# GpSimd makes the sign and tail bits of converted weights, VectorE joins them in one step; reciprocals go into x; two buffers for keys-values

## The chip, the cores and the metric

The kernel runs on one core of a Trainium2 chip. The metric is the time of one execution on the device in microseconds (us). The engines are named as in the profile: PE is TensorE (PEld its weight loads), DVE is VectorE, ACT is ScalarE, POOL is GpSimd, SP is SyncE, from whose queue all DMA transfers start.

## The reference

Attention with random features for 8 batches of 8 heads, sequence 576, head size 64, 128 features, and on its output a dense layer pair with an unusual gate:

```python
def phi(x):                       # for q and k, both scaled by 64 ** -0.25
    proj = einsum('bhsd,md->bhsm', x, omega)
    h = proj - sum(x * x, -1) / 2
    return exp(h - max(h, -1)) / sqrt(128)
q_p, k_p = phi(q), phi(k)
kv  = einsum('bhsm,bhsd->bhmd', k_p, v)
z   = sum(k_p, 2)
out = (q_p @ kv) / (q_p @ z + 1e-6)          # per head

x = out.transpose(0, 2, 1, 3).reshape(4608, 512)
h = x @ w_in                                  # 512 x 2048
g = h * erf(softplus(h))
y = g @ w_out                                 # 2048 x 512
```

The two weight matrices arrive as float64.

## The kernel before

**Order of the work.** `build` does not write instructions; it lists operations (`pl.op`) with the tiles that they read and write, the engines that may run them (T for PE, A, V, G, S), a cost for each, and for some a planned time. `Plan.order` then plays these costs through a list scheduler on the host and so fixes one order for each engine, in which the instructions are issued. An operation starts on an engine when its inputs are ready, its tiles find a free buffer (`SLOTS` per pool, `CAPS` per stream) and it is the one with the earliest due time. The third number of an option is a limit: an engine takes the operation only while its due time is at least so far away (-1e9: always). So `GATES0 = 10` and `RESTS0 = 15` mean that in the first batches GpSimd takes the work called gate only if it is due in 10 us or later and rest only in 15 or later; VectorE takes both always. On PE, matmuls with 64 rows (names that begin with proj) and key-values (kv, 64 columns) form groups: after one of these, another of the same kind that is due within `NEAR = 12` us goes first, if its tiles have room (lines 236 to 241). One PSUM bank holds one `ps` tile; there are eight, and the attention stream may hold six (`att=6`).

**Attention.** It goes by pairs of heads, 32 in all. The first four pairs are done singly (`first`), the others two pairs at a time (`attention`, 14 times), spread over the dense layers of the batch before. For two pairs: three projections of keys (tile `ppk`, nine chunks of 128 rows in three groups; each group takes two banks), maximum on VectorE (`sqk`, `mxk`), exponential on ScalarE (`fk`), then both pairs' key-values (`kvp`), then the same for queries (`ppq`, `fq`), transposes (`pt` to `qh`, `ql`), and the matmuls `nd`, which give numerator and denominator. The squares of q and k (`unq`, `unk`) are squared and folded mostly on GpSimd. Key-values are copied out of PSUM to `kh` and, from pair 12 on (counted from 0), their rest to `kl`; each has one buffer. Last (`attend`), ScalarE takes the reciprocal of the denominator by Ln and Exp into `rc` (two buffers), and VectorE multiplies the numerator by it into `xs` (four buffers, 128 multiplications of 64x288).

**Float32 in two parts.** Matmuls after attention run on pairs of reduced-precision numbers, a high part and the rest, three matmuls for a product (`xh`, `xl`; `gh`, `gl`; the two halves of `w`). From batch 2 on, the first dense layer uses a Strassen-like scheme with seven products and sums of weights (`R`, `S`, `cS`).

**Weights.** There are 32 units of 128x512 weights. `make` loads one as 64-bit words (tile `st`, low and high 32 bits), turns it into float32 by handling the bits, splits it into high part and rest (tile `w`) and stores it to DRAM (`wdw`), from which later uses fetch it. The steps for a unit before the change:

- `w_bias` on GpSimd or ScalarE: the high word, read as float32, times 2^-112, into tile `wt` (in SBUF);
- `w_shift` on VectorE: `wt` shifted left by 3 into the PSUM tile `pw`;
- `w_sign` and `w_tail` on VectorE, both in place on `pw`: the sign bit of the high word and the top three bits of the low word are put in;
- `w_high` (ScalarE or VectorE) and `w_rest` (VectorE): the two parts.

`pw` has one bank (`PW = 1`). `wt` lies in the pool of the tiles `gh`, whose buffers have room for 4,608 bytes per partition.

Of the kernel before, what the change touches and what calls it, by code (L numbers as in the profile page):

```python
# [10 lines left out]
F32 = mybir.dt.float32  # L11
F32R = mybir.dt.float32r
I32 = mybir.dt.int32
AF = mybir.ActivationFunctionType
ALU = mybir.AluOpType
AX = mybir.AxisListType
# [3 lines left out]
P = 128  # L20
# [7 lines left out]
T = 288  # L28
# [7 lines left out]
HW = 2 * BW  # L36
# [21 lines left out]

COST = dict(mm=0.132, proj=0.224, turnout=0.40, tr=0.109, kv=1.08, table=1.3)
LAG = {"T": 0.35, "A": 0.35, "V": 0.33, "G": 0.33, "S": 0.3}  # L60
SLOTS = dict(w=8, u=2, un=2, f=2, mx=2, sq=2, v=2, qh=1, ql=1, kh=1, kl=1, rc=2, xs=4, xh=2, xl=2, u2=2,
             hs=4, gs=2, gh=6, gl=6, os=4, ps=8)
CAPS = dict(st=2, wt=2, cv=2, att=6, moe1=3, moe2=2)

# [25 lines left out]
class Plan:  # L90
# [44 lines left out]
    def order(self, slots, caps):  # L135
# [46 lines left out]
        def can(o):  # L182
            for t in o.uses:
                if t.slot is None and t.users[0] is not o:
                    return False
            more, room = {}, {}
            for t in o.alloc:
                k = more.get(t.stream, 0)
                stream = self.streams[t.stream]
                if stream[min(nxt[t.stream] + k, len(stream) - 1)] is not t:  # L190
                    return False
                if len(free[t.pool]) <= room.get(t.pool, 0):
                    return False
                if held[t.stream] + k >= (t.cap or caps.get(t.stream, 99)):
                    return False
                more[t.stream], room[t.pool] = k + 1, room.get(t.pool, 0) + 1
            return True
# [5 lines left out]
        while True:  # L203
            progress = True
            while progress:
                progress = False
                for e in engines:
# [28 lines left out]
                    if e == "T" and half and chosen.half != half:  # L236
                        near = [x for x in ready[e] if x[2].half == half and x[2].start is None
                                and x[0] < now + NEAR and can(x[2])]
                        if near:
# [95 lines left out]
EARLYB = 7  # L335
PW = 1
WHV = 0.0
GATES0 = 10.0
RESTS0 = 15.0
SQA = 4.0  # L340
NEAR = 12.0
KV1 = 0.15
GROUPS = ((0, 3), (3, 6), (6, 9))
WHG = 5.0
WBG = -1e9


def build(emit):

    pl = Plan()  # L350
    E = emit
# [17 lines left out]
    def when(n, x):  # L369
        return pair_time(n, x) if n < NP else quad_time(n // 2, x)  # L370

    xh, xl = {}, {}
# [26 lines left out]
    def make(u, t):  # L399

        nm = "_".join(str(c) for c in u)
        st = pl.tile("gl", f"st{nm}", [P, HW, 2], I32, "st")
        pl.op("wload", [("S", 0.1, AHEAD)], lambda e: E.w_load(st, u),
              writes=[(st, 0), (t, "room")], size=P * HW * 8)
        w = pl.tile("gh", f"wt{nm}", [P, HW], I32, "wt")
        pl.op("wbias", [("G", 0.65, WBG), ("A", 0.6, -1e9)], lambda e: E.w_bias(e, st, w),
              reads=[(st, 0)], writes=[(w, 0)])

        p = pl.tile("ps", f"pw{nm}", [P, HW], I32, "pw", PW)
        pl.op("wshift", [("V", 0.7, -1e9)], lambda e: E.w_shift(p, w), reads=[(w, 0)],  # L410
              writes=[(p, 0)])
        pl.op("wsign", [("V", 0.7, -1e9)], lambda e: E.w_sign(st, p), reads=[(st, 0), (p, 0)],
              writes=[(p, 0)])
        pl.op("wtail", [("V", 0.72, -1e9)], lambda e: E.w_tail(st, p), reads=[(st, 0), (p, 0)],
              writes=[(p, 0)])
        parts(t, lambda: p.ap.bitcast(F32).rearrange("p (k c) -> p k c", k=2), [(p, 0)], True)
        store(u, t)

    def unit(u, block=None):
# [3 lines left out]
                    [P, 2 if block is None else 1, 2, BW], F32R,  # L423
                    cap=SLOTS["w"] - CAPS["cv"] if clock[0] < starts[2 * PLAIN + 1] else None)
        if u not in stored:
# [45 lines left out]
    xs = {}  # L471
# [3 lines left out]
    def early(n):  # L475
        return EARLYB if n < NP else None
# [132 lines left out]
    def attend(n, t0):  # L609
        a = pairs[n]  # L610
        x = xs[n] = pl.tile("xs", f"xs{a['nm']}", [P, 2, T])
        for t in range(2):
            rc = pl.tile("rc", f"rc{a['nm']}_{t}", [P, T])
            nds = []
            for j in range(2):
                nd = pl.tile("ps", f"nd{a['nm']}_{j}_{t}", [P, 512], F32, "att", early(n))
                nds.append(nd)
                c = range((j * S + t * T) // 384, (j * S + (t + 1) * T - 1) // 384 + 1)
                pl.op("nd", [("T", 0.5 if n < WHOLE else 3 * COST["mm"], -1e9)],
                      lambda e, j=j, t=t, nd=nd: E.attend(nd, a["kh"], a["kl"], a["qh"], a["ql"], j, t),  # L620
                      reads=[(a["kh"], 0), (a["kl"], 0)] + [(a["qh"], i) for i in c]
                      + [(a["ql"], i) for i in c], writes=[(nd, 0)],
                      plan=when(n, t0 + 0.1 * t + 0.05 * j))
            opts = [("V", 0.93, -1e9), ("A", 1.45, RECIP)] if n < POW else [("A", 1.5, -1e9)]
            pl.op("recip", opts, lambda e, nds=nds, rc=rc: E.reciprocal(e, rc, nds),
                  reads=[(nd, 0) for nd in nds], writes=[(rc, 0)], set="exp")
            for j in range(2):
                pl.op("divide", [("V", 0.4, -1e9)],
                      lambda e, j=j, t=t, nd=nds[j], rc=rc: E.divide(x, nd, rc, j, t),
                      reads=[(nds[j], 0), (rc, 0)], writes=[(x, (j, t))])  # L630

    def split(b, c):

# [116 lines left out]
    def chain(b, ph, fps):  # L750
# [13 lines left out]
        for fp, g in zip(fps, gr):  # L764
            four = [(g["hs"], (i, t)) for i in range(2) for t in range(2)]
            pl.op("gate", [("V", 1.27, -1e9), ("G", 2.78, GATES if (b, ph) >= EARLY else GATES0)], lambda e, g=g: E.gate(e, g["gs"], g["hs"]),
                  reads=four + [(g["gs"], 0)], writes=four)
# [3 lines left out]
            g["gl"] = pl.tile("gl", f"gl{b}_{ph}_{fp}", [P, 2, 2, T], F32R, cap=4 if b < PLAIN or (b, ph) == (PLAIN, 0) else None)  # L771
            pl.op("rest", [("G", 2.95, RESTS if (b, ph) >= EARLY else RESTS0), ("V", 1.3, -1e9)],
                  lambda e, g=g: E.rest(e, g["gl"], g["hs"], g["gh"]),
# [66 lines left out]
def tile_attention_moe(ctx: ExitStack, tc: tile.TileContext, qT, kT, qN, kN, vP, omT, w1, w2, out):  # L840
# [6 lines left out]
    class InOrder:  # L847
# [5 lines left out]
        def __getattr__(self, name):  # L853
            method = getattr(self.engine, name)

            def call(*args, **kwargs):
# [3 lines left out]
    pe, act, dve, pool, sp = (InOrder(e) for e in (nc.tensor, nc.scalar, nc.vector, nc.gpsimd,  # L860
                                                   nc.sync))
# [10 lines left out]
    eps = const.tile([P, 1], F32, name="eps")  # L872
# [13 lines left out]
    def copy(e, dst, src):  # L886
        if e == "A":
            act.activation(dst, src, AF.Copy)
        elif e == "G":
# [15 lines left out]
    class Emit:  # L905
# [4 lines left out]
        def w_load(self, t, u):  # L910
            src = w1[u[1], u[2]] if u[0] == "1" else w2[u[1], u[2], u[3]]
            sp.dma_start(t.ap.rearrange("p a b -> p (a b)"), src.bitcast(I32))

        def w_bias(self, e, t, w):
            dst, src = w.ap.bitcast(F32), t.ap[:, :, 1].bitcast(F32)
            if e == "A":
                act.activation(dst, src, AF.Copy, scale=2.0 ** -112)
            else:
                pool.tensor_scalar(dst, src, 2.0 ** -112, 0.0, op0=ALU.mult, op1=ALU.add)

        def w_shift(self, p, w):
            dve.tensor_scalar(p.ap, w.ap, 3, None, op0=ALU.logical_shift_left)

        def w_sign(self, t, w):
            dve.scalar_tensor_tensor(w.ap, t.ap[:, :, 1], -2 ** 31, w.ap,
                                     op0=ALU.bitwise_and, op1=ALU.bitwise_or)

        def w_tail(self, t, w):
            dve.scalar_tensor_tensor(w.ap, t.ap[:, :, 0], 29, w.ap,
                                     op0=ALU.logical_shift_right, op1=ALU.bitwise_or)  # L930

        def w_high(self, e, t, src):
            copy(e, t.ap[:, :, 0, :], src())
# [21 lines left out]
        def pair_square(self, e, u, qk, i, parts):  # L955
# [5 lines left out]
            else:  # L961
                act.activation(u.ap[dst, c], u.ap[src, c], AF.Square)

# [17 lines left out]
        def square(self, e, un):  # L981
            if e == "A":
                act.activation(un.ap, un.ap, AF.Square)
            else:
# [27 lines left out]
        def exponential(self, parts):  # L1012
            for f, c, m, pp, k in parts:
                act.activation(f.ap[:, c, :], pp.ap[:, k * P:(k + 1) * P], AF.Exp, bias=m)

# [48 lines left out]
        def reciprocal(self, e, rc, nds):  # L1064

            for j, nd in enumerate(nds):
                num, den = rows(j)
                if e == "A":
                    act.activation(rc.ap[num], nd.ap[den, :T], AF.Ln, bias=eps[den])
                else:  # L1070
                    dve.tensor_scalar(rc.ap[num], nd.ap[den, :T], 1e-6 * P, -1.0, op0=ALU.add,
                                      op1=ALU.pow)
            if e == "A":
                act.activation(rc.ap, rc.ap, AF.Exp, scale=-1.0)

        def divide(self, x, nd, rc, j, t):
            num = rows(j)[0]
            dve.tensor_mul(x.ap[num, t, :], nd.ap[num, :T], rc.ap[num])

        def x_high(self, e, h, src, i, n):  # L1080
            copy(e, h.ap[:, i:i + n, :], src())
# [51 lines left out]
    plan = build(Emit())  # L1133
    slots = dict(SLOTS)
    for o in plan.ops:
# [60 lines left out]
```

## Time and profile before

| | us |
|---|---|
| median of 3 runs | 1037.3 |
| lowest and highest run | 1034.58, 1037.31 |
| the profiled execution | 1036.85 |
| its span, first to last instruction | 1035.1 |

| engine | busy us | share of the span | instructions |
|---|---|---|---|
| PE | 1015.7 | 98% | 8784 |
| DVE | 750.2 | 72% | 1488 |
| ACT | 686.9 | 66% | 1312 |
| POOL | 495.8 | 48% | 479 |

The mean granted clock of TensorE is 0.995 of full speed. Matmuls are pipelined and their ends are modelled, so PE counts as busy also where it runs below its best pace. In the groups of the profile all the instructions of the kernel have one line (the line that issues the planned operations), so that groups are told apart by tiles: `pw<-st,pw` is the step that writes `pw` from `st` and `pw`.

### The profile page before, as it was taken

What the parts mean: (1) busy time and instruction counts of PE and PEld (TensorE: products, weight loads), DVE (VectorE), ACT (ScalarE), POOL (GpSimd) and SP (SyncE); (2) the same over time, 40 slices, a digit from 0 to 9 for tenths busy, and PEclk for the clock granted to TensorE, in tenths of its full rate; (3) what the DMA queues carried; (4) which work ended last, traced back from release to release, by engine and by line L of the source; (5) the groups of instructions that cost most, each with busy time, mean ns of one, the idle gap of its engine ahead of it and who ended that gap; (6) DMA issues with size and microseconds to landing.
All of it is one profiled execution on the core that took longest, in us unless ns stands there. A gap on an engine that the chain in (4) does not pass through costs nothing.

```text
span 1035.1 us, 23091 instructions
## 1 busy us (share of the span) xinstructions
PE 1015.7 (98%) x8784; PEld 983.8 (95%) x8784; DVE 750.2 (72%) x1488; ACT 686.9 (66%) x1312; POOL 495.8 (48%) x479
## 2 busy tenths in 40 slices
PE   7989999999999999999999999999999999999998
PEld 6789899999999999999999999999999999999998
DVE  3989999989777577875777766776778756765531
ACT  7869959867786665777667666775668666453340
POOL 4637828969775233833446234652428312433310
PEclk9989999999999999999999999999999999999999
DMA  7675879789768686677777676778766756668861
GB/s 230 193 242 208 262 247 343 274 312 351 238 241 290 245 286 220 242 235 268 262 253 249 217 269 239 243 263 268 265 207 232 254 178 224 225 233 265 277 229 47
DMA packets 80142, 254.18 MB, mean 246 GB/s; under 512 B 8992, under 2 KB 9504, under 8 KB 80032
## 3 DMA queue, kind: packets, MB, share of 16 engines
q1 hardware_dynamic: 80032, 252.71, 71.3%
q8 instruction: 70, 1.15, 0.4%
q14 instruction: 40, 0.33, 0.1%
HBM read 218.07 MB, written 34.60 MB: 244 GB/s over the span
## 4 chain that ended last, share of the span: by engine, by line
PE 89%; DVE 5%; ACT 3%; issue 1%; DMA 1%; SPq 1%; POOL 0%; ACTq 0%; DVEq 0%
PE o L857 38%; PE hS L857 15%; PE hA L857 11%; PE h L857 9%; PE nd L857 4%; PE kvp L857 3%; PE ppk L857 3%; PE ppq L857 3%; PE pt L857 3%; DVE pw L857 1%; DVE xs L857 1%; DMA uq<-qT 1%; SPq L857 1%; DVE w L857 1%; ACT fq L857 1%
## 5 line engine op out<-in xcount | busy, mean ns | idle before, releaser
L857 PE MATMUL o<-gh,w 128*128 128x288 f32 x2048 | 446.2, 299 | 1.0 <-DVE w L857 0.9
L857 PEld LDWEIGHTS o<-gh,w 128*128 128x128 f32 x2048 | 338.7, 188 | 7.4 <-DVE w L857 1.4
L857 PE MATMUL o<-gl,w 128*128 128x288 f32 x1024 | 302.0, 295 | 0.0
L857 PEld LDWEIGHTS o<-gl,w 128*128 128x128 f32 x1024 | 192.7, 188 | 0.6 <-DVE gl L857 0.3
L857 POOL TENSOR_TENSOR hs<-gs,hs 128x576 f32<-128x576 f32 x70 | 107.5, 1557 | 169.8 <-ACT gs L857 126.2
L857 PE MATMUL hS<-xh,wS 128*128 128x288 f32 x768 | 187.8, 298 | 0.0
L857 POOL TENSOR_TENSOR gl<-hs,gh 128x576 fp32r<-128x576 f32 x84 | 138.0, 1668 | 40.1 <-ACT gh L857 31.0
L857 PE MATMUL hA<-xh,w 128*128 128x288 f32 x576 | 147.3, 297 | 0.0
L857 PEld LDWEIGHTS hS<-xh,wS 128*128 128x128 f32 x768 | 134.5, 188 | 0.7
L857 PE MATMUL h<-xh,w 128*128 128x288 f32 x512 | 120.0, 311 | 0.5 <-DVE w L857 0.2
L857 ACT ACT_TABLE_LOAD x92 | 118.0, 1283 | 2.4 <-PEq L1187 0.7
L857 POOL TENSOR_TENSOR unq<-unq 128x288 f32<-128x288 f32 (+2 forms) x63 | 50.3, 801 | 137.2 <-ACT unq L857 122.3
L857 PE MATMUL hS<-xl,wS 128*128 128x288 f32 x384 | 113.4, 295 | 0.0
L857 PEld LDWEIGHTS hA<-xh,w 128*128 128x128 f32 x576 | 103.2, 188 | 0.0
L857 ACT ACTIVATE fk<-ppk,mxk 128x128 f32<-128x128 f32 x288 | 77.3, 416 | 37.6 <-DVE mxk L857 37.4
L857 ACT ACTIVATE rc<-nd,eps 64x288 f32<-64x288 f32 x128 | 63.5, 496 | 54.5 <-PE nd L857 48.2
L857 PEld LDWEIGHTS h<-xh,w 128*128 128x128 f32 x512 | 86.9, 191 | 3.4 <-DVE w L857 0.7
L857 PE MATMUL hA<-xl,w 128*128 128x288 f32 x288 | 85.3, 296 | 0.0
L857 POOL TENSOR_TENSOR unk<-unk 128x144 f32<-128x144 f32 (+2 forms) x68 | 50.5, 747 | 70.9 <-DMA unk<-kN 50.5
L857 ACT ACTIVATE gs<-hs 128x1152 f32<-128x1152 f32 x64 | 72.4, 1162 | 18.1 <-DVE hs L857 17.5
L857 ACT ACTIVATE fq<-ppq,mxq 128x128 f32<-128x128 f32 x288 | 79.4, 392 | 6.4 <-DVE mxq L857 6.3
L857 PE MATMUL h<-xl,w 128*128 128x288 f32 x256 | 76.3, 298 | 0.0
(109 smaller groups left out, 2058.3 us busy)
## 6 DMA issues: line engine op xcount, KB each, us to landing
w<-wdw SPq DMA_DIRECT2D x176, 512.0 KB, 4.6
wS<-wdcS SPq DMA_DIRECT2D x96, 512.0 KB, 4.5
st<-w SPq DMA_DIRECT2D x32, 512.0 KB, 4.8
wdw<-w SPq DMA_DIRECT2D x32, 512.0 KB, 4.1
w<-wdw SPq DMA_DIRECT2D x48, 256.0 KB, 3.9
v<-vP SPq DMA_DIRECT2D x32, 325.0 KB, 6.2
out<-os SPq DMA_DIRECT2D x32, 288.0 KB, 3.8
wdcS<-cS SPq DMA_DIRECT2D x16, 512.0 KB, 4.6
```

What stands on the lines that cost most here:

```text
L857: return tc.keep_in_program_order(method(*args, **kwargs))
```

## The change

- **Weights.** `w_bias` runs on GpSimd alone. The new `w_tail` (GpSimd) reads the top byte of the low word and computes byte / 32 - 15.5 / 32, which rounds to the top three bits as a number, into the low int16 half of a second plane of `wt`; the new `w_sign` (GpSimd) writes 0 or -2^15 into the high int16 half. `w_shift` becomes one VectorE instruction: plane 0 shifted left by 3, or plane 1, into `pw`. `wt` is twice as long and still fits its buffer.
- **Reciprocals.** `rc` goes away; the reciprocal is written into the place in `xs` that the multiplication then overwrites.
- **Buffers.** `kh` and `kl` get two each.
- **Planner.** `GATES0` 10 to 3, `RESTS0` 15 to 5, `NEAR` 12 to 20, and the new operations' costs.

```diff
@@ -11,6 +11,8 @@
 F32 = mybir.dt.float32
 F32R = mybir.dt.float32r
 I32 = mybir.dt.int32
+U8 = mybir.dt.uint8
+I16 = mybir.dt.int16
 AF = mybir.ActivationFunctionType
 ALU = mybir.AluOpType
 AX = mybir.AxisListType
@@ -58,7 +60,7 @@
 
 COST = dict(mm=0.132, proj=0.224, turnout=0.40, tr=0.109, kv=1.08, table=1.3)
 LAG = {"T": 0.35, "A": 0.35, "V": 0.33, "G": 0.33, "S": 0.3}
-SLOTS = dict(w=8, u=2, un=2, f=2, mx=2, sq=2, v=2, qh=1, ql=1, kh=1, kl=1, rc=2, xs=4, xh=2, xl=2, u2=2,
+SLOTS = dict(w=8, u=2, un=2, f=2, mx=2, sq=2, v=2, qh=1, ql=1, kh=2, kl=2, xs=4, xh=2, xl=2, u2=2,
              hs=4, gs=2, gh=6, gl=6, os=4, ps=8)
 CAPS = dict(st=2, wt=2, cv=2, att=6, moe1=3, moe2=2)
 
@@ -335,14 +337,15 @@
 EARLYB = 7
 PW = 1
 WHV = 0.0
-GATES0 = 10.0
-RESTS0 = 15.0
+GATES0 = 3.0
+RESTS0 = 5.0
 SQA = 4.0
-NEAR = 12.0
+NEAR = 20.0
 KV1 = 0.15
 GROUPS = ((0, 3), (3, 6), (6, 9))
 WHG = 5.0
 WBG = -1e9
+WTAIL = (("G", 0.66, WBG),)
 
 
 def build(emit):
@@ -402,16 +405,16 @@
         st = pl.tile("gl", f"st{nm}", [P, HW, 2], I32, "st")
         pl.op("wload", [("S", 0.1, AHEAD)], lambda e: E.w_load(st, u),
               writes=[(st, 0), (t, "room")], size=P * HW * 8)
-        w = pl.tile("gh", f"wt{nm}", [P, HW], I32, "wt")
-        pl.op("wbias", [("G", 0.65, WBG), ("A", 0.6, -1e9)], lambda e: E.w_bias(e, st, w),
+        w = pl.tile("gh", f"wt{nm}", [P, 2, HW], I32, "wt")
+        pl.op("wbias", [("G", 0.65, WBG)], lambda e: E.w_bias(e, st, w),
               reads=[(st, 0)], writes=[(w, 0)])
+        pl.op("wtail", WTAIL, lambda e: E.w_tail(e, st, w),
+              reads=[(st, 0)], writes=[(w, 1)])
+        pl.op("wsign", [("G", 0.68, WBG)], lambda e: E.w_sign(st, w),
+              reads=[(st, 0)], writes=[(w, 2)])
 
         p = pl.tile("ps", f"pw{nm}", [P, HW], I32, "pw", PW)
-        pl.op("wshift", [("V", 0.7, -1e9)], lambda e: E.w_shift(p, w), reads=[(w, 0)],
-              writes=[(p, 0)])
-        pl.op("wsign", [("V", 0.7, -1e9)], lambda e: E.w_sign(st, p), reads=[(st, 0), (p, 0)],
-              writes=[(p, 0)])
-        pl.op("wtail", [("V", 0.72, -1e9)], lambda e: E.w_tail(st, p), reads=[(st, 0), (p, 0)],
+        pl.op("wshift", [("V", 0.7, -1e9)], lambda e: E.w_shift(p, w), reads=[(w, 0), (w, 1), (w, 2)],
               writes=[(p, 0)])
         parts(t, lambda: p.ap.bitcast(F32).rearrange("p (k c) -> p k c", k=2), [(p, 0)], True)
         store(u, t)
@@ -610,7 +613,6 @@
         a = pairs[n]
         x = xs[n] = pl.tile("xs", f"xs{a['nm']}", [P, 2, T])
         for t in range(2):
-            rc = pl.tile("rc", f"rc{a['nm']}_{t}", [P, T])
             nds = []
             for j in range(2):
                 nd = pl.tile("ps", f"nd{a['nm']}_{j}_{t}", [P, 512], F32, "att", early(n))
@@ -622,12 +624,12 @@
                       + [(a["ql"], i) for i in c], writes=[(nd, 0)],
                       plan=when(n, t0 + 0.1 * t + 0.05 * j))
             opts = [("V", 0.93, -1e9), ("A", 1.45, RECIP)] if n < POW else [("A", 1.5, -1e9)]
-            pl.op("recip", opts, lambda e, nds=nds, rc=rc: E.reciprocal(e, rc, nds),
-                  reads=[(nd, 0) for nd in nds], writes=[(rc, 0)], set="exp")
+            pl.op("recip", opts, lambda e, nds=nds, t=t: E.reciprocal(e, x.ap[:, t, :], nds),
+                  reads=[(nd, 0) for nd in nds], writes=[(x, (j, t)) for j in range(2)], set="exp")
             for j in range(2):
                 pl.op("divide", [("V", 0.4, -1e9)],
-                      lambda e, j=j, t=t, nd=nds[j], rc=rc: E.divide(x, nd, rc, j, t),
-                      reads=[(nds[j], 0), (rc, 0)], writes=[(x, (j, t))])
+                      lambda e, j=j, t=t, nd=nds[j]: E.divide(x, nd, j, t),
+                      reads=[(nds[j], 0)], writes=[(x, (j, t))])
 
     def split(b, c):
 
@@ -911,23 +913,26 @@
             src = w1[u[1], u[2]] if u[0] == "1" else w2[u[1], u[2], u[3]]
             sp.dma_start(t.ap.rearrange("p a b -> p (a b)"), src.bitcast(I32))
 
+        def scaled(self, e, dst, src, scale, bias):
+            if e == "A":
+                act.activation(dst, src, AF.Copy, scale=scale, bias=bias)
+            else:
+                pool.tensor_scalar(dst, src, scale, bias, op0=ALU.mult, op1=ALU.add)
+
         def w_bias(self, e, t, w):
-            dst, src = w.ap.bitcast(F32), t.ap[:, :, 1].bitcast(F32)
-            if e == "A":
-                act.activation(dst, src, AF.Copy, scale=2.0 ** -112)
-            else:
-                pool.tensor_scalar(dst, src, 2.0 ** -112, 0.0, op0=ALU.mult, op1=ALU.add)
+            self.scaled(e, w.ap[:, 0].bitcast(F32), t.ap[:, :, 1].bitcast(F32), 2.0 ** -112, 0.0)
+
+        def w_tail(self, e, t, w):
+            byte = t.ap.bitcast(U8).rearrange("p a b -> p (a b)")[:, 3::8]
+            self.scaled(e, w.ap[:, 1].bitcast(I16)[:, 0::2], byte, 1 / 32, -15.5 / 32)
+
+        def w_sign(self, t, w):
+            pool.tensor_scalar(w.ap[:, 1].bitcast(I16)[:, 1::2], t.ap[:, :, 1].bitcast(F32), 0.0, -2.0 ** 15,
+                               op0=ALU.is_lt, op1=ALU.mult)
 
         def w_shift(self, p, w):
-            dve.tensor_scalar(p.ap, w.ap, 3, None, op0=ALU.logical_shift_left)
-
-        def w_sign(self, t, w):
-            dve.scalar_tensor_tensor(w.ap, t.ap[:, :, 1], -2 ** 31, w.ap,
-                                     op0=ALU.bitwise_and, op1=ALU.bitwise_or)
-
-        def w_tail(self, t, w):
-            dve.scalar_tensor_tensor(w.ap, t.ap[:, :, 0], 29, w.ap,
-                                     op0=ALU.logical_shift_right, op1=ALU.bitwise_or)
+            dve.scalar_tensor_tensor(p.ap, w.ap[:, 0], 3, w.ap[:, 1], op0=ALU.logical_shift_left,
+                                     op1=ALU.bitwise_or)
 
         def w_high(self, e, t, src):
             copy(e, t.ap[:, :, 0, :], src())
@@ -1066,16 +1071,16 @@
             for j, nd in enumerate(nds):
                 num, den = rows(j)
                 if e == "A":
-                    act.activation(rc.ap[num], nd.ap[den, :T], AF.Ln, bias=eps[den])
+                    act.activation(rc[num], nd.ap[den, :T], AF.Ln, bias=eps[den])
                 else:
-                    dve.tensor_scalar(rc.ap[num], nd.ap[den, :T], 1e-6 * P, -1.0, op0=ALU.add,
+                    dve.tensor_scalar(rc[num], nd.ap[den, :T], 1e-6 * P, -1.0, op0=ALU.add,
                                       op1=ALU.pow)
             if e == "A":
-                act.activation(rc.ap, rc.ap, AF.Exp, scale=-1.0)
-
-        def divide(self, x, nd, rc, j, t):
+                act.activation(rc, rc, AF.Exp, scale=-1.0)
+
+        def divide(self, x, nd, j, t):
             num = rows(j)[0]
-            dve.tensor_mul(x.ap[num, t, :], nd.ap[num, :T], rc.ap[num])
+            dve.tensor_mul(x.ap[num, t, :], nd.ap[num, :T], x.ap[num, t, :])
 
         def x_high(self, e, h, src, i, n):
             copy(e, h.ap[:, i:i + n, :], src())
```

## The prediction

> **What bounds the kernel now.** I read the page first, then busy time by stretch, then the timeline and waits where TensorE pauses, then the chain of waits. Busy time on the page, and PE's, PEld's, DVE's, ACT's and POOL's in a stretch from the middle (start and end, length, busy time and count of each engine, granted clock, DMA share, GB/s):
>
> ```profile
> PE 1015.7 (98%) x8784; PEld 983.8 (95%) x8784; DVE 750.2 (72%) x1488; ACT 686.9 (66%) x1312; POOL 495.8 (48%) x479
> ```
> ```profile
> 400.00:500.00 100.00, 100.00 (x913) 97.55 (x912) 74.32 (x156) 66.82 (x135) 43.78 (x41) 1.00 0.74 250
> ```
>
> PE has 1035.1 − 1015.7 = 19.4 us idle in the whole span, and none in the middle. A freer VectorE is worth nothing there, unless PE itself executes less. Two places remain: the early part, where weights are made, and the price of PE's own order. The early part, 26 to 246 us, in which all 32 weight units are converted:
>
> ```profile
> 26.00:60.00 34.00, 28.63 (x266) 25.14 (x262) 32.84 (x68) 28.17 (x81) 22.30 (x30) 0.97 0.61 198
> 60.00:110.00 50.00, 49.94 (x431) 46.81 (x430) 44.52 (x94) 41.90 (x87) 30.64 (x33) 0.95 0.68 228
> 110.00:160.00 50.00, 48.33 (x443) 43.98 (x443) 47.05 (x91) 38.99 (x92) 27.45 (x33) 1.00 0.81 264
> 160.00:210.00 50.00, 49.44 (x409) 46.69 (x406) 47.71 (x73) 42.80 (x78) 43.79 (x39) 1.00 0.86 312
> 210.00:246.00 36.00, 36.00 (x357) 34.79 (x355) 31.29 (x62) 25.30 (x58) 26.73 (x29) 1.00 0.93 340
> ```
>
> VectorE is the fullest helper: 32.84 + 44.52 + 47.05 + 47.71 + 31.29 = 203.4 of 220 us, against 150.9 for GpSimd. PE is idle for 5.4 + 0.1 + 1.7 + 0.6 + 0 = 7.7 us. The clock costs more, which no idle column shows: 0.03 × 34 + 0.05 × 50 = 3.5 us of PE work. So the stretch can give back 11.2 us at most.
>
> Is VectorE the cause? Its timeline at the worst point, PE's longest waits in the first 70 us (total, times, longest), and two ten-microsecond stretches:
>
> ```profile
> 50.61 0.69 DVE L857 TENSOR_SCALAR pw<-wt 128x512 int32<-128x512 int32 x1
> 51.33 1.43 DVE L857 SCALAR_TENSOR_TENSOR pw<-st,pw 128x512 int32<-128x512 int32 x2
> 52.80 0.69 DVE L857 CAST w<-pw 128x512 fp32r<-128x512 f32 x1
> 53.52 0.69 DVE L857 TENSOR_TENSOR w<-pw,w 128x512 fp32r<-128x512 f32 x1
> 54.13 0.93 DVE L857 TENSOR_TENSOR xs<-nd,rc 64x288 f32<-64x288 f32 x2
> ```
> ```profile
> PE ppk L857 <- DVE xs L857: 2.1, 2, 1.2
> PE kvp L857 <- ACT fq L857: 1.9, 2, 1.6
> PE ppk L857 <- DVE w L857: 0.7, 1, 0.7
> ```
> ```profile
> 50.00:60.00 10.00, 7.20 (x52) 6.04 (x52) 9.53 (x19) 6.39 (x16) 6.05 (x9) 0.90 0.60 209
> 60.00:70.00 10.00, 10.00 (x126) 9.26 (x125) 7.73 (x21) 4.93 (x16) 0.35 (x1) 0.76 0.72 226
> ```
>
> The divisions (xs), which free PSUM banks for the key projections (ppk), stand on VectorE behind five weight steps of one unit. PE's two ppk waits on VectorE, 2.1 + 0.7 = 2.8 us, are the whole idle time of 50 to 60 us, and the half-rate clock that costs 1.0 + 2.4 = 3.4 us between 50 and 70 goes with that pause. So 6.2 of the 11.2 us hang on VectorE at one place.
>
> **The weight steps.** VectorE's and GpSimd's groups between 20 and 320 us (count, busy time, mean in ns, idle before):
>
> ```profile
> L857 DVE SCALAR_TENSOR_TENSOR pw<-st,pw 128x512 int32<-128x512 int32 x64 | 44.4, 694 | 1.8
> L857 DVE TENSOR_TENSOR xs<-nd,rc 64x288 f32<-64x288 f32 x49 | 22.2, 453 | 1.2 <-ACT rc L857 0.2
> L857 DVE TENSOR_SCALAR pw<-wt 128x512 int32<-128x512 int32 x32 | 22.0, 687 | 3.2 <-POOL wt L857 1.9 <-ACT hs L857 1.0
> ...
> L857 DVE TENSOR_TENSOR R<-w 128x512 f32<-128x512 f32 x7 | 8.5, 1239 | 0.1
> ```
> ```profile
> L857 POOL TENSOR_SCALAR wt<-st 128x512 f32<-128x512 f32 x21 | 15.4, 735 | 16.0 <-DMA st<-w 12.4 <-DVE pw L857 3.1
> ```
>
> Removed from VectorE: 22.0 + 44.4 = 66.4 us in 96 instructions. Added: 32 joins. No row shows one with both operands in SBUF. From below I bound it by the same instruction with one operand in PSUM, 694 ns; from above by the addition of the same size with two SBUF operands, R, 1239 ns. That is 22.2 to 39.6 us, so VectorE gets 26.8 to 44.2 us back. I take 35, halfway: POOL, which R would have to wait for, is idle for a third of the stretch. The Trainium skill has a rule against this change, on its page SBUF — State Buffer, section "SBUF: two separate sides": VectorE and GpSimd share one pair of ports as an exclusive lock, which a VectorE operation with two SBUF inputs takes, and the loser blocks for the whole instruction. R's 545 ns over the PSUM form agree with it; by it alone VectorE's gain would lie at the 26.8 us end, with as much waiting on GpSimd.
>
> Added on POOL: the tail and sign bits, 64 steps. The nearest row is wt, the same elements from the same strided source: 735 ns, so 47.0 us. Output of half the width may make it less and a blocked port more; 0.5 to 1.24 us each bounds it. The 32 − 21 = 11 conversions that ran on ScalarE add 8.1 us. POOL goes from 150.9 to about 206 of 220 us and becomes what VectorE was. The planner can answer, since gates and rests run on either engine and VectorE's freed 35 us can take them; the lower limits for them in the first batches (10 to 3 and 15 to 5) pull the other way, as they let GpSimd take such work nearer to its due time. The join now waits for three POOL steps, and behind a waiting join stand divisions, maxima and the splits, for which PE waits.
>
> What it gives: in 50 to 58 us three steps, 0.69 + 1.43 = 2.1 us, become 0.7 to 1.2, so divisions start 0.9 to 1.4 us earlier at each unit that stands in front of them, and 2 of the 2.8 us go. If the pause shrinks so far, the half-rate stretch may not come; at a little over even odds I count 2 of its 3.4 us. Of the 1.7 idle in 110 to 160 I count 1. Against these 5 us I charge 1 us for units that now come later. Net 4; the bounds are 11.2 gained and, below nothing, rival 3's price.
>
> **Two buffers for keys-values.** This acts where PE is full. The chain (start, length, matmuls in a row), and what VectorE waits for when it copies keys-values (kh) out of PSUM:
>
> ```profile
> 68.37 1.54 PE ppq L857 x24
> ...
> 347.60 2.46 PE kvp L857 x72
> ...
> 353.06 5.17 PE o L857 x39
> 358.24 1.54 PE ppq L857 x24
> 359.78 4.16 PE o L857 x30
> 363.94 0.87 PE ppq L857 x12
> ...
> 827.90 2.21 PE ppk L857 x36
> ...
> 847.33 1.54 PE ppq L857 x24
> ```
> ```profile
> DVE kh L857 <- PE nd L857: 24.9, 10, 2.5
> ```
>
> In each of the 14 two-pair attentions, from the first to the last ppq row shown, the 36 query projections run in pieces: 24, main work, 12 (in one, three times 12). Twelve more cost 1.54 − 0.87 = 0.67 us, so a piece has 0.20 us of its own, and the x36 row agrees: 1.54 + 0.67 = 2.21. The main work behind a piece pays too: at 5.17 / 39 = 0.1326 us, 30 take 3.98, not 4.16. A second piece therefore costs 0.20 + 0.18 = 0.38 us of PE time, in which PE counts as busy.
>
> Why not 36 at once? Each third takes two of the six PSUM banks that attention may hold. Both pairs' key-values are multiplied together (x72), but with one kh buffer the second pair's cannot be copied out until the first pair's nd matmuls are done; that is the wait of kh for nd. It holds a bank all through the query projections: four for two thirds, one for it, and the last third finds one. With two buffers all six are there: up to 14 × 0.38 = 5.3 us; I take 13 of them, 5. The key projections are mostly split as well, but the nd banks of the pair before hold them up, so I count nothing; if the wider grouping (12 to 20) merges them, 5.3 more is the other bound.
>
> **The rest.** The reciprocal written into x takes no instruction away: the divisions keep one PSUM and one SBUF operand. One of x's four buffers is claimed a reciprocal earlier; the long stretch between two pairs' attentions hides that, and if not, ScalarE waits with the exponentials behind it.
>
> **Sum.** The profiled execution took 1036.85 us for its span of 1035.1; the median of the runs is 1037.3. 1036.85 − 4 − 5 = 1028. A measurement can tell about 0.3%, 3.1 us, from no change, so below 1034.2 is faster and above 1040.4 slower.
>
> **Rivals.**
> 1. *Only the merging pays.* The early pauses move to the next late thing, the exponentials: ACT is busy 28.17 of the first 34 us and PE's 1.9 us for fq are its. Against it stand the named waits for VectorE. 1036.85 − 5 = 1032. Chance 0.22.
> 2. *It doesn't do what it says.* The order comes from a list scheduler, which may give the freed bank to other work and leave the queries in pieces. For it: even now, without a bank held by kvp, keys are split. With the early 4 us it is 1033, without 1037. Chance 0.16, half each.
> 3. *GpSimd becomes the bound: slower.* Its place is 160 to 210 us, where POOL is busy 43.79 of 50 and VectorE's weight work on tile pw is:
>
> ```profile
> 160.00:210.00 50.00, 19.95 (x29) 1.56 (x3) 1.00 0.86 312
> ```
>
> A unit has four VectorE steps there and a copy that is VectorE's half of the time, so 29 / 4.5 = 6.4 units. POOL gets 6.4 × (2 + 11/32) × 0.735 = 11 us more, 55 in 50. It decides once the planner can't move those 5 us of gates to VectorE in time. If each join and a POOL step also block each other for R's 0.545 us, 3.5 more, PE waits 8.5 us for weights and a half-rate stretch like the one above adds 3.4: 1036.85 − 5 + 11.9 = 1044. Against it: VectorE has more than that free. Chance 0.14.
> 4. *Everything pays*: the early 11.2 but 3, all queries and half the keys: 1036.85 − 8.2 − 5.3 − 2.7 = 1021. Chance 0.08.
>
> **How the numbers follow.** The forecast keeps 0.40. Faster: 0.38 of that, 0.16 of rival 1, 0.06 of rival 2 and rival 4: 0.68. Slower: rival 3 where the merging doesn't cover it, 0.12. The remaining 0.20 is within 0.3%. The range, 1019 to 1037, takes in rival 4, the forecast with its early term between 0 and 9, and rivals 1 and 2; it leaves out rival 3 and the tails.
>
> **What would show it.** Right: 32 joins of 0.7 to 1.2 us in place of 96 steps; 96 POOL wt steps near 0.7; in 26 to 246 us DVE below 180 and POOL about 200; ppq x36 in the chain in ten attentions or more, and kh no longer waiting for nd; PEclk 1.00 between 50 and 70. Wrong: ppq still x24; PE waiting for w between 60 and 250; joins well over 1.24 us; a lower clock in more stretches than now.

## The result and the profile after

The changed kernel takes 1066.8 us (median of 4 runs, 1066.33 to 1067.39) against 1037.3 before: a ratio of 1.0291, 95% interval 1.0272 to 1.0309, slower, where 1028 was forecast. The profiled execution took 1066.33 us for a span of 1064.5, 29.4 us more than before. Its busy times, then the stretches of the weights' conversion as they were shown before:

```profile
PE 1027.0 (96%) x8784; PEld 992.7 (93%) x8784; DVE 720.7 (68%) x1424; ACT 678.7 (64%) x1316; POOL 599.6 (56%) x536
```
```profile
26.00:60.00 34.00, 25.92 (x213) 21.53 (x211) 22.62 (x47) 25.07 (x69) 32.43 (x33) 0.95 0.57 194
60.00:110.00 50.00, 49.01 (x406) 45.08 (x406) 39.77 (x82) 33.72 (x74) 41.11 (x40) 0.90 0.57 202
110.00:160.00 50.00, 38.18 (x304) 34.95 (x302) 29.50 (x56) 30.79 (x65) 48.12 (x40) 0.86 0.56 186
160.00:210.00 50.00, 48.38 (x419) 45.50 (x420) 40.27 (x69) 35.61 (x77) 48.01 (x44) 0.97 0.74 262
210.00:246.00 36.00, 33.28 (x246) 30.75 (x245) 30.33 (x52) 21.50 (x40) 34.95 (x26) 1.00 0.74 266
```

The whole loss stands in these five rows. PE's idle time is 8.1 + 1.0 + 11.8 + 1.6 + 2.7 = 25.2 us where it was 7.7, and the clock below 1 costs 0.05 x 34 + 0.10 x 50 + 0.14 x 50 + 0.03 x 50 = 15.2 us where it was 3.5. Together that is 29.2 us more, against 29.4 in the span; 17 of it lie between 110 and 160 us. POOL is full (204.6 of 220 us) and VectorE is down to 162.5, near the 206 and 168 of the forecast, but by luck: the steps that make `wt` take 123.5 us of POOL instead of the 70.5 forecast, other work of POOL moved behind 246 us, and VectorE's figure is low also because it stands waiting (with a quick sign step, below, it is 187.9). Why PE does worse, the new steps show (GpSimd's and VectorE's groups between 20 and 320 us):

```profile
L859 POOL TENSOR_SCALAR wt<-st 128x512 int16<-128x512 f32 x32 | 70.3, 2198 | 0.1
L859 POOL TENSOR_SCALAR wt<-st 128x512 f32<-128x512 f32 x32 | 27.8, 870 | 8.1 <-DMA st<-w 5.8
...
L859 POOL TENSOR_SCALAR wt<-st 128x512 int16<-128x512 uint8 x32 | 25.4, 795 | 2.1
```
```profile
L859 DVE SCALAR_TENSOR_TENSOR pw<-wt 128x512 int32<-128x512 int32 x32 | 25.5, 797 | 41.1 <-POOL wt L859 40.9
```

Scaling (f32 to f32) and tail bits (uint8 to int16) cost about what the prediction took. The sign step (f32 to int16) takes 2198 ns, three times as much; the shortest of the 32 takes 2086, so waiting for a port now and then is not the reason. And the join, itself cheap, has 40.9 us of VectorE standing idle in front of it. What that does, on GpSimd, VectorE, then PE:

```profile
119.30 8.20 POOL L859 TENSOR_SCALAR wt<-st 128x512 f32<-128x512 f32 x6
...
122.89 0.70 DVE L859 SCALAR_TENSOR_TENSOR pw<-wt 128x512 int32<-128x512 int32 x1 [4.62 <-POOL wt L859]
```
```profile
124.28 0.40 PE L859 MATMUL o<-gh,w 128*128 128x288 f32 x1 [0.84 <-ACT w L859]
...
126.50 0.53 PE L859 MATMUL o<-gh,w 128*128 128x288 f32 x2 [1.68 <-DVE w L859]
```

Two units' six steps take GpSimd 8.2 us where the planner counted 2 x (0.65 + 0.66 + 0.68) = 4.0. VectorE has reached the first join and stands 4.6 us with everything behind it; then PE waits 0.84 and 1.68 us for the parts of `w`. What stands behind a join in VectorE's queue comes late too, such as the copy of transposed queries (`qh`) at 153.32 us, for which PE then waits 1.9 us:

```profile
152.50 0.70 DVE L859 SCALAR_TENSOR_TENSOR pw<-wt 128x512 int32<-128x512 int32 x1 [2.39 <-POOL wt L859]
...
153.93 1.72 PE L859 MATMUL nd<-qh,kh 128*128 128x288 f32 x6 [1.93 <-DVE qh L859]
```

The second term, in the chain of waits:

```profile
74.42 2.21 PE ppq L859 x36
...
376.89 2.46 PE kvp L859 x72
387.50 2.21 PE ppq L859 x36
...
620.10 2.46 PE kvp L859 x72
632.59 1.54 PE ppq L859 x24
...
865.66 2.46 PE kvp L859 x72
```

Queries run whole in seven of the 14 attentions, most of them in the middle, but from 630 us in pieces again. From the key-values at 376.89 to those at 865.66 it takes 488.8 us. The same eight attentions took 836.67 - 347.60 = 489.1 before, by these rows and the one at 347.60 shown with the prediction:

```profile
592.36 2.46 PE kvp L857 x72
...
836.67 2.46 PE kvp L857 x72
```

So where PE is full the change gives 0.3 us. The first four of the eight, whose queries run whole, take 620.10 - 376.89 = 243.2 us instead of 592.36 - 347.60 = 244.8, a gain of 1.6 or 0.39 for each, about the 0.38 that the prediction had put on a piece; the last four lose most of it again.

### The profile page after: what moved, and what is told of

Its sections match the earlier page's. It is cut to its first block, busy times and chain, and to the rows that moved or that the text cites. A ratio compares the mean times of both kernels' runs of the same rounds, so it can differ in the third digit from the quotient of the medians.

```text
span 1064.5 us, 23069 instructions
## 1 busy us (share of the span) xinstructions
PE 1027.0 (96%) x8784; PEld 992.7 (93%) x8784; DVE 720.7 (68%) x1424; ACT 678.7 (64%) x1316; POOL 599.6 (56%) x536
## 3 DMA queue, kind: packets, MB, share of 16 engines
q8 instruction: 70, 1.15, 0.4%
## 4 chain that ended last, share of the span: by engine, by line
PE 81%; POOL 13%; issue 2%; DVE 1%; DMA 1%; SPq 1%; ACT 0%; POOLq 0%; ACTq 0%; DVEq 0%
PE o L859 36%; PE hS L859 14%; PE hA L859 11%; POOL wt L859 7%; PE h L859 5%; PE nd L859 4%; PE ppk L859 3%; PE kvp L859 3%; PE ppq L859 3%; PE pt L859 2%; POOL gl L859 2%; POOL unq L859 1%; POOL hs L859 1%; POOL unk L859 1%; SPq L859 1%
## 5 line engine op out<-in xcount | busy, mean ns | idle before, releaser
L859 POOL TENSOR_TENSOR hs<-gs,hs 128x576 f32<-128x576 f32 x74 | 120.2, 1646 | 179.3 <-ACT gs L859 135.4
L859 POOL TENSOR_SCALAR wt<-st 128x512 f32<-128x512 f32 (+2 forms) x96 | 122.6, 1288 | 10.3 <-DMA st<-w 5.8
L859 POOL TENSOR_TENSOR unq<-unq 128x288 f32<-128x288 f32 (+2 forms) x66 | 54.2, 821 | 123.8 <-ACT unq L859 90.2
L859 ACT ACTIVATE xs<-nd,eps 64x288 f32<-64x288 f32 x128 | 63.5, 496 | 48.2 <-PE nd L859 45.9
```

The costliest lines, as they stand in the source:

```text
L859: return tc.keep_in_program_order(method(*args, **kwargs))
```

## The experiments

Theory A: one instruction, the compare on GpSimd, is three times as long as planned, and the loss is its. Theory B: three GpSimd steps, the shared port and the looser limits overload GpSimd whatever the sign step costs. The first three kernels tell them apart. Times are medians; the kernel before took 1036.7 to 1037.0 beside them.

**Sign step by multiply and add:**

```diff
-            pool.tensor_scalar(..., t.ap[:, :, 1].bitcast(F32), 0.0, -2.0 ** 15, op0=ALU.is_lt, op1=ALU.mult)
+            pool.tensor_scalar(..., t.ap[:, :, 1].bitcast(F32), 0.0, 0.0, op0=ALU.mult, op1=ALU.add)
```

> The changed kernel with the sign step's compare-and-multiply replaced by a multiply-and-add by zero, same operands, shapes and order of work; it leaves the signs of the weights out. Theory A (the compare itself is slow on GpSimd, 2.12 us where 0.68 was planned, and that one instruction is the loss): the step falls to 0.65 to 0.8 us, VectorE's 40.9 us of waiting for wt falls under 10, and the time to 1024 to 1032. Theory B (three GpSimd steps, the shared port and the looser limits overload GpSimd in any case): the time stays above 1045. Theory C (it is the conversion of float32 to int16 or its stride that is slow, not the compare): the step stays at 2.1 us and the time at 1067.

Measured: 1037.57 us, ratio to before 1.0005 (0.9996 to 1.0015). The step fell to this:

```profile
L859 POOL TENSOR_SCALAR wt<-st 128x512 int16<-128x512 f32 x32 | 31.0, 968 | 0.1
```

VectorE's wait for wt fell from 40.9 to 8.5 us. The same operands, types and strides take a median of 0.79 us instead of 2.12, so it is the operation; conversion and stride (theory C) are out, and so is theory B, which had the time above 1045. The step carries 29 us, the whole loss against before. But the time is that of before, above the 1024 to 1032 expected: without the slow step the change still gives nothing.

**Sign step by minimum and multiply**, which saturates:

```diff
-            ..., 0.0, -2.0 ** 15, op0=ALU.is_lt, op1=ALU.mult)
+            ..., 0.0, 2.0 ** 60, op0=ALU.min, op1=ALU.mult)
```

> The changed kernel with the sign step as a minimum with 0 and a multiplication by 2^60, whose result saturates in int16: no compare that makes a truth value. If only such compares are slow on GpSimd, the step takes 0.65 to 0.8 us and the time equals that of the multiply-and-add run within 2 us; if the two-operation form with anything but multiply and add is slow, it stays near 2.1 us and the time near 1067.

Measured: 1070.94 us, ratio 1.0326 (1.0306 to 1.0345).

```profile
L859 POOL TENSOR_SCALAR wt<-st 128x512 int16<-128x512 f32 x32 | 70.2, 2195 | 2.0
```

With a minimum as its first operation the step is as slow as with a compare. Of the three forms tried only multiply and add is quick.

**Sign bit on VectorE again**, GpSimd doing scale and tail:

```diff
-        pl.op("wsign", [("G", 0.68, WBG)], lambda e: E.w_sign(st, w),
-              reads=[(st, 0)], writes=[(w, 2)])
...
+        pl.op("wsign", [("V", 0.7, -1e9)], lambda e: E.w_sign(st, p), reads=[(st, 0), (p, 0)],
+              writes=[(p, 0)])
```

> The changed kernel with the sign bit put in on VectorE again, as one more step on pw after the join; tail and scaling stay on GpSimd, now a full int32 plane. Theory A: GpSimd loses 70 us of sign steps, VectorE gets 22 us, the time is 1028 to 1034, since PE waits no more for late joins. Theory B: about 1045, since two GpSimd steps still precede each join under the looser limits. Tail into int32 should take 0.65 to 0.8 us as it does into int16.

Measured: 1034.49 us, ratio 0.9984 (0.9969 to 0.9999); the tail took 0.79 us on average into int32 too. It agrees with theory A about the sign, and again falls short of 1028, just outside the range expected.

**Merging alone**: two buffers, reciprocal in x, look-ahead 20, weights and limits as before.

> The kernel before with only the two kh and kl buffers, the reciprocal in x and the wider grouping; weights and limits as before. Theory A with the prediction's second term: 12 or 13 query projections in one piece, 1031 to 1033. Rival, from the changed kernel's chain, in which the queries run whole in 6 of 14 attentions and the keys come in more pieces late: nothing or up to 2 us gained, 1035 to 1038.

Measured: 1028.07 us, ratio 0.9914 (0.9889 to 0.9939), the fastest kernel of the study. More than expected; so the next three take it apart. Look-ahead back to 12:

```diff
-NEAR = 20.0
+NEAR = 12.0
```

> The merge-only kernel with the grouping's look-ahead back at 12: two buffers of kh and kl and the reciprocal in x alone. If the freed bank is what lets the queries run whole, as the prediction had it, most of the 8.9 us remains: 1027 to 1030, with ppq x36 in ten attentions or more. Rival: the wider look-ahead does it, and this is 1034 to 1037.

Measured: 1038.15 us, ratio 1.0008 (0.9993 to 1.0022), above both ranges expected. The look-ahead alone, in the kernel before:

> The kernel before with the look-ahead of 20 and nothing else. With the bank as the cause, 1035 to 1038 and ppq still x24 and x12; with the look-ahead as the cause, 1028 to 1031.

Measured: 1035.62 us, ratio 0.9989 (0.9977 to 1.0002), and its queries stay in pieces to the end:

```profile
786.09 1.54 PE ppq L857 x24
836.17 2.46 PE kvp L857 x72
846.83 1.54 PE ppq L857 x24
```

Look-ahead 16 with the buffers:

> The merge-only kernel with a look-ahead of 16 in place of 20, which gives the same order up to about 107 us and another after it. At 20 it gained 8.9 us, at 12 nothing, with the queries whole in both. If the gain belongs to the look-ahead, this lies between, 1031 to 1035. If 20 and 12 differ by one pause that an order meets or misses, it lies near one of them: 1027 to 1030 without a pause at 180 to 220 us, 1036 to 1040 with one.

Measured: 1035.58 us, ratio 0.9991 (0.9979 to 1.0003). Here is the stretch 210 to 246 us of the merge-only kernel with 20, 12 and 16:

```profile
210.00:246.00 36.00, 36.00 (x347) 35.08 (x346) 30.27 (x51) 29.78 (x67) 30.06 (x29) 1.00 0.88 326
```
```profile
210.00:246.00 36.00, 31.00 (x273) 28.40 (x271) 31.55 (x58) 28.28 (x67) 19.05 (x21) 0.91 0.74 264
```
```profile
210.00:246.00 36.00, 31.85 (x284) 29.38 (x281) 31.54 (x58) 27.04 (x65) 17.52 (x20) 0.91 0.72 255
```

At 12 the pause costs 5.0 idle + 0.09 x 36 = 3.2 of clock, 8.2 of the 10.1 us between the two; at 16 it costs 7.4 of 7.5, and its time lies just outside all the ranges expected. In both PE waits 3.8 us for w from VectorE there. The order with 20 has no such pause. So the buffers, with the reciprocal in x, do let queries run whole (8 of 14 with them at 12, none without them at 20), and one pause takes at 12 and 16 what 20 keeps.

The pause does not explain the 8.9 us themselves, because the kernel before has none there either (36.00 us busy at clock 1.00, in the prediction's rows). Of the 9.9 us between the two profiled executions (spans of 1035.1 and 1025.2), 1.9 lie in the eight attentions, by these rows of the merge-only kernel:

```profile
339.44 2.46 PE kvp L859 x72
...
826.66 2.46 PE kvp L859 x72
```

The other 8 lie ahead of them, where PE stands idle for 13.0 us instead of 15.8 and runs at half clock for a shorter time. Why this order waits less there stays open.

The eight attentions also test the prediction's price for a piece, for in each kernel PE executes the same 4368 matmuls in them. A piece too many is one that a group of 36 projections would not need. Counted in the timelines, for queries and keys together:

| kernel | pieces too many | the eight attentions, us | gained | at 0.38 us a piece |
|---|---|---|---|---|
| before | 8 + 7 | 489.1 | | |
| changed | 5 + 9 | 488.8 | 0.3 | 0.4 |
| buffers, look-ahead 12 | 3 + 7 | 487.4 | 1.7 | 1.9 |
| merge-only, 20 | 3 + 6 | 487.2 | 1.9 | 2.3 |
| merge-only, 16 | 0 + 4 | 484.9 | 4.2 | 4.2 |

The price holds, to within 0.5 us in 13 of the 14 kernels; the minimum kernel, with 5 + 9 pieces too many, takes 490.1. What differs from kernel to kernel is how many pieces the order leaves.

**The limits.** The new ones in the merge-only kernel, then (the reverse edit) the old ones in the multiply-and-add kernel:

```diff
-GATES0 = 10.0
-RESTS0 = 15.0
+GATES0 = 3.0
+RESTS0 = 5.0
```

> The merge-only kernel (weights as before) with the limits of the change, 3 and 5. Theory D: the looser limits cost here too, 1033 to 1038. Theory E: GpSimd has room in this kernel (222 of 320 us busy), so 1027 to 1030.

Measured: 1030.38 us, ratio 0.9929 (0.9907 to 0.9951).

> The multiply-and-add kernel (it leaves the signs of the weights out) with the gate and rest limits of before, 10 and 15. It came out 9.5 us over the merge-only kernel. Theory D: those 9.5 us are the looser limits, which fill GpSimd with gates and rests in front of weight steps; then this is 1027 to 1031. Theory E: they are the three GpSimd steps in front of each join, whatever the limits; then it stays at 1035 to 1039.

Measured: 1037.3 us, ratio 1.0002 (0.9992 to 1.0013). Theory D falls: the limits move 2.3 us in one kernel and nothing in the other.

**VectorE's relief for nothing.** The kernel before, sign and tail steps planned but not issued:

```diff
         def w_sign(self, t, w):
-            dve.scalar_tensor_tensor(w.ap, t.ap[:, :, 1], -2 ** 31, w.ap, ...)
+            pass
         def w_tail(self, t, w):
-            dve.scalar_tensor_tensor(w.ap, t.ap[:, :, 0], 29, w.ap, ...)
+            pass
```

> The kernel before in its own planned order, with VectorE's sign and tail steps not issued, so that signs and last bits of the weights are left out: 64 x 0.694 = 44 us of VectorE work gone between 26 and 246 us and nothing added anywhere. This is the relief that the change was to bring, for free. If VectorE's load sets PE's early losses, as the prediction had it, 5 to 11 us are gained: 1026 to 1032. Rival: PE's early losses follow from single late links and from the order, not from VectorE's load, and 0 to 3 us are gained: 1034 to 1037.

Measured: 1033.41 us, ratio 0.9972 (0.9961 to 0.9983), 3.3 us.

```profile
60.00:110.00 50.00, 49.74 (x441) 46.60 (x441) 35.03 (x73) 42.38 (x88) 33.06 (x35) 0.98 0.71 241
110.00:160.00 50.00, 49.10 (x478) 44.99 (x475) 35.91 (x76) 40.43 (x89) 27.30 (x33) 1.00 0.82 285
```

VectorE is busy 70.9 of these 100 us instead of 91.6, and PE's pauses hardly change: over the five stretches its idle time goes from 7.7 to 6.6 us, and the clock costs 3.7 instead of 3.5. The gain lies between the two ranges expected, close to the smaller one. A new order that knows of the relief might use it better; none was run.

**The planner told the truth.** The changed kernel with measured costs (the edit shown), then the multiply-and-add kernel with old limits and its own measured costs, 0.91, 0.79 and 0.97:

```diff
-WTAIL = (("G", 0.66, WBG),)
+WTAIL = (("G", 0.79, WBG),)
...
-        pl.op("wbias", [("G", 0.65, WBG)], ...
+        pl.op("wbias", [("G", 0.87, WBG)], ...
...
-        pl.op("wsign", [("G", 0.68, WBG)], ...
+        pl.op("wsign", [("G", 2.2, WBG)], ...
```

> The changed kernel with the planner told what the three GpSimd steps take, 0.87, 0.79 and 2.2 in place of 0.65, 0.66 and 0.68. Theory F (the loss is joins that come later than planned, while VectorE's queue stands): VectorE's 40.9 us of waiting for wt falls under 15 and the time to 1038 to 1048. Theory G (the loss is GpSimd's 48 us of extra work, which no plan removes): 1055 to 1067.

Measured: 1042.73 us, ratio to before 1.0066 (1.0051 to 1.0081): of the 30 us of loss 24 go, although GpSimd still runs the slow step 32 times. VectorE's wait, and the eight attentions:

```profile
DVE pw L859 <- POOL wt L859: 4.0, 5, 1.3
```
```profile
355.90 2.46 PE kvp L859 x72
...
840.99 2.46 PE kvp L859 x72
```

PE's idle time and slow clock between 26 and 246 us fall from 40.4 to 22.7 us. Besides, all 14 queries run whole, and the eight attentions take 485.1 us instead of 488.8.

> The multiply-and-add kernel with the old limits (signs of the weights left out), with the planner told the steps' measured means, 0.79, 0.91 and 0.97. It was 9 us over the merge-only kernel, with VectorE waiting 9.6 us for wt. Theory F: that wait falls to 3 or less and the time to 1028 to 1033. Theory H (orders scatter by several us, whatever the wait): the wait falls and the time stays at 1034 to 1039.

Measured: 1031.77 us, ratio 0.9959 (0.9946 to 0.9972), 5.5 us under the same kernel with planned costs; the wait for wt is 1.9 us instead of 9.6. But most of the gain is not that wait's. The eight attentions, with planned and with measured costs:

```profile
347.77 2.46 PE kvp L859 x72
...
836.94 2.46 PE kvp L859 x72
```
```profile
345.82 2.46 PE kvp L859 x72
...
830.90 2.46 PE kvp L859 x72
```

They take 485.1 us instead of 489.2, because the new order leaves 4 pieces too many instead of 14. Between 26 and 246 us PE's idle time and slow clock go only from 15.3 to 14.0 us. So theory F holds for the slow step: what costs there is a step that comes later than the order assumes, with VectorE's queue standing behind it. For the quick step it is not shown. For theory G, GpSimd's extra work under a plan that knows it, there remain 6 us over the kernel before, or 14.7 over the merge-only kernel.

## Why the prediction was wrong, point by point

One mis-priced step turned the forecast gain of 9 us into a loss of 29. Without that step the time is 1037.6, so the two gains of 4 and 5 us did not come either; points 3 and 5 tell why.

1. *64 steps on POOL at wt's 735 ns.* This is the step that failed. Half of them, the tail, took 795 ns; the signs took 2198. The row it was taken from does a multiply and an add, and the new step a compare; same shape and stride did not make it the nearest row. Neither bound, 0.5 or 1.24 us, came from a compare on GpSimd, and what happened lay outside both.
2. *Rival 3, GpSimd becomes the bound.* Right in direction, wrong in mechanism and size (1044). It had POOL overrun its time from 160 to 210 us; the loss lies mostly at 110 to 160, and comes through VectorE's queue, which stands behind each waiting join. The prediction named this wait ("behind a waiting join stand divisions, maxima and the splits") and charged PE 1 us for it; VectorE stood idle for 40.9 us, and PE lost 29. That the planner could move gates away was true (told the true costs, it leaves POOL 567 us of work instead of 600), but it didn't know that there was need.
3. *VectorE's load sets the early losses: 5 us before the charge, at most 11.2.* Too high, for the order as it was planned. With 44 us of VectorE work left out and nothing put in its place, 3.3 us come back. With a quick sign step 8.5 us of waiting for wt are left, and the time is that of before; that these waits, of joins for three GpSimd steps, use up the 3.3 us is argued, not shown. A busy share of 92% and two named waits showed VectorE late at one place, not that its load was the limit.
4. *The join.* 797 ns mean, within 694 to 1239, with a median of 700 and a longest of 1919. The longest ones agree with the Trainium skill's rule on the exclusive port pair (SBUF — State Buffer, "SBUF: two separate sides"): the two of 1890 and 1919 ns began during a GpSimd subtraction and ended 0.56 us after it. That costs 0.1 us a join on average here. The price falls on GpSimd as well, which the sum left out: eight scaling steps that began 0.05 us after a join had begun took 1.15 to 1.17 us, where the shortest takes 0.64.
5. *Queries merge in 12 or 13 of 14 attentions: 5 us.* The mechanism and the price of a piece were right: VectorE's 24.9 us of waiting for nd before a copy to kh are gone, queries run whole with the buffers and not without them, and 0.38 us a piece fits the table above. (The reciprocal in x came with the buffers and was not tried alone.) The count failed: in the changed kernel seven of the 14 run whole, and of the late keys more are cut up than before, so that 14 of 15 pieces remain and 0.3 us is left over eight attentions. For the keys the prediction counted nothing, and as a bound only a gain. The order decides: the same work with measured costs keeps all 14 whole and gains 4.0 us there. What in the order cuts them up late was not tried.
6. *The clock.* That half-rate time follows PE's pauses held: 15.2 us below full clock with 25.2 idle, 3.5 with 7.7. Each microsecond of pause went with about half a microsecond more. The prediction had it as a loss only in rival 3, with 3.4 us.

What stays open: why the multiply-and-add kernel, even with true costs, is 3.7 us above the merge-only kernel, although its eight attentions are 2.1 us shorter. Kernels that differ by a single planner number differ by 7.5 to 10 us, so such a remainder can't be put down to any one part.

## What to carry to other kernels

Before an operation is moved to another engine, its price has to come from a row with the same operation on that engine; shape, type and stride are not enough. Where a planner fixes an in-order queue from costs, a wrong cost can hurt more than the work itself (here 24 of 30 us), since everything behind the early-placed instruction stands, so measured durations go into the table first. Whether an engine that is 92% busy is the bound can be tried by leaving its work out in the same order, which here would have said 3 us before any rewriting. And when kernels with different orders are compared, a stretch with the same work in each, like the eight attentions, tells apart what an idea gives and what the order adds or takes.

## What the runs showed of the hardware

GpSimd's two-operation instruction on 128x512 float32 into int16 took a median of 0.79 us with multiply and add, and 2.12 us with is_lt and multiply or with min and multiply, on the same operands. A uint8 source cost no more than a float32 one at the same step of 8 bytes: 0.78 us into int16, and 0.66 into 32 bits as against 0.67.
